# The eighth head pair's exponents transposed by DMA instead of TensorE, with a new search of the order of work

## The chip, the cores and the metric

The kernel runs on one core of a Trainium2 chip. The metric is device microseconds for one execution of the whole program. Before the change it takes 604.61 us, the median of 3 runs (604.5 to 605.64).

## The reference, cut to what matters

```python
# attention with memory: B, H, S, D = 4, 8, 576, 64
scores = q @ k.T / sqrt(D), causal;  a = exp(scores - max) / sum
local  = a @ v
mem    = phi(q) @ M_prev / (phi(q) . z_prev + 1e-6)     # phi = elu + 1
attn   = g * mem + (1 - g) * local                      # g = sigmoid(beta), one per head
# expert: 2304 tokens, d_model 512, d_ff 1536
x   = attn, heads side by side
out = (sigmoid(x @ w_gate) * (x @ w_val)) @ w_out
```

All results are wanted to float32 accuracy; the expert's weights arrive as float64 bit patterns.

## The kernel before, in words

**Groups and pairs.** The 2304 tokens are cut into six groups of 384. Group 0 holds the last 192 tokens of batches 0 and 1, groups 1 to 4 the first 384 tokens of one batch each, group 5 the last 192 of batches 2 and 3. Each group has four pairs of heads, so there are 24 pairs, n = 0 to 23; the eighth pair, n = 7, is the last of group 1. For each pair TensorE makes the scores (`heads`, line 534, and the memory's terms, line 491), VectorE masks them and finds the row extremes (line 603), ScalarE takes the exponents (line 612). A pair of groups 1 to 4 has two items: item 0 of 256 columns and item 1 of 512 columns (384 and 128), each for two heads. The exponents `a` must then be transposed into `at` (`turn`), multiplied with the values (`values`, line 732; two pairs in one step in groups 1 to 4, so pairs 6 and 7 go together), scaled, added to the memory's part, and the result `x` transposed once more (`across`) to feed the expert.

**Two ways to transpose.** Pairs below `XBAR` = 8 use TensorE: 128x128 transposes into PSUM (line 296) and a ScalarE copy from there (line 302). Pairs from `XBAR` on use `planes`: VectorE copies the float32 tile so that its lower and upper 16-bit halves lie apart (line 662), SyncE issues a DMA transpose of 16-bit elements (line 667), and VectorE puts the halves together again (line 662). The same switch decides how `across` transposes `x`.

**Expert.** Every matrix is split into a high and a low part in FP32R, and three products are made for each (line 289). There are 12 blocks of 128 hidden units. Stages: group 0 with blocks 0 to 5, group 1 with blocks 5 to 0, group 0 with blocks 6 to 11, group 1 with 11 to 6, then groups 2 to 5 with all 12. A block has 24 products of 384 columns over four 128-row slices of `x` (slice kd comes from pair kd of the group; in the first block of a stage slice 3 is taken last), a `gate` step (lines 992, 994, 302, 312) and 9 products of 512 columns (`down`). Converting a block's weights from float64 bits takes three conversions of four VectorE and two ScalarE steps each (`convert`; line 881 is the last integer step of each).

**Order.** The program is first written down as 4,634 steps with their dependencies. `Program.issue` then lays each engine's instructions in an order found from planned costs: at each point an engine takes, of its steps that are ready, the one with the lowest number. The number is the step's place in the program, less a `LEAD`, plus what the table `MOVED` adds to it. The order is fixed at build time; on the chip each engine runs its list in that order and waits where a step's inputs are late. For a DMA transpose the plan counts 1.3 us of SyncE, then 1.2 us and the transfer at 380 KB per us, then 0.95 us until an engine may start. At most six `a` and four `at` tiles exist.

**End.** In group 5 the last stage finishes three tiles of 128 rows in the order 2, 0, 1. Tile 2 is halved by ScalarE (line 1037) and goes out in two transfers, tile 0 is halved by VectorE (line 1040), both on SyncE's queue; tile 1 comes in two halves of 256 columns, added up by VectorE (line 1021) and sent by SyncE and ScalarE (line 1024).

Of the kernel before, what the change touches and what calls it, by code (L numbers as in the profile page):

```python
# [11 lines left out]
U16 = mybir.dt.uint16  # L12
AF = mybir.ActivationFunctionType
ALU = mybir.AluOpType
# [5 lines left out]

VC = 66

XBAR = 8

AHEAD = 8

# [11 lines left out]
LINK = 380.0, 1.2  # L38

MOVED = {  # L40
# [42 lines left out]
}  # L83

PE = 2
# [121 lines left out]
def tile_attention_memory_moe(  # L207
# [9 lines left out]
    nc = tc.nc  # L217
    B, HP, _, _ = qk.shape
    D, H = 64, 2 * HP
    NT, DM = out.shape  # L220
# [5 lines left out]
    NG = NT // GT  # L226
# [5 lines left out]
    pg = Program()  # L232
# [65 lines left out]
    def act(n, emit, r, w):  # L298
        pg.add("act", 0.102 + n / 1200.0, emit, r, w)
# [4 lines left out]
    def dve(n, emit, r, w, fast=False):  # L304
        pg.add("dve", 0.083 + n / (1920.0 if fast else 960.0), emit, r, w)
# [99 lines left out]
    for g in range(NG):  # L405
        for p in range(HP):
            u = Pair()
# [248 lines left out]
        recall(n, [(t[:, end:end + 3 * MC].rearrange("p (c j x) -> p c j x", c=3, j=1), k, j, j + 1)  # L656
                   for j, (t, k) in enumerate(sp[0])])

    def planes(src, pl, tl, dst, W, r, pk, lk, key, more=()):

        def move(o, i, r, w):
            dve(2 * W, lambda: nc.vector.tensor_copy(out=o, in_=i), r, w, fast=True)  # L662

        pl, tl = pl[:, :2 * W], tl[:, :2 * W]
        src, dst = (t.bitcast(U16).rearrange("p (w two) -> p two w", two=2) for t in (src, dst))
        move(pl.rearrange("p (two w) -> p two w", two=2), src, r, [pk])
        pg.add("sp", 1.3, lambda: nc.sync.dma_start_transpose(
            out=tl.rearrange("p (x q) -> p x q", q=128), in_=pl), [pk], [lk, *more], 0.75 * W)
        move(dst, tl.rearrange("p (two w) -> p two w", two=2), [lk, *more], [key])

    def crossed(a, nb, at, k):


        W = 128 * nb
        keys = []
        for j, (t, ks, ak) in enumerate(a):
            key = k + (j,)
            o = at[:, W * j:W * j + W]
            end = [ak + ("pad",)] * (nb == 5)
            planes(t[:, :W], o.bitcast(U16), t[:, :W].bitcast(U16), o, W, ks + end, key, ks[0], key, ks[1:] + end)  # L680
            keys.append(key)
            if end:
                pad(t, ak)
        return keys

    def turn(n, c):
        u = pairs[n]
        a = u.a.pop(c)
        nb = -(-sum(W for _, _, W in u.items[c]) // 128)
        at, k = at_r.take()  # L690
        if XBAR <= n:
            u.at[c] = (at, crossed(a, nb, at, k), nb)
            return
        blocks = [(j, i) for j in range(2) for i in range(nb)]
        keys = []
# [246 lines left out]
    def moe(n):  # L942
# [72 lines left out]
        for t in order:  # L1015
# [13 lines left out]
            if not opens:  # L1029
# [3 lines left out]
                for r, q, m in rows(g, t):  # L1033
                    load(out[r:r + m, :], o[q:q + m], 2.1 * m, [ob_k], [])
                continue
            if g < NG - 1 or t != order[1]:
                act(DM, lambda o=o, acc=acc: nc.scalar.activation(
                    out=o, in_=acc, func=AF.Copy, scale=0.5), [acc_k], [ob_k])
            else:
                dve(DM, lambda o=o, acc=acc: nc.vector.tensor_scalar(  # L1040
                    out=o, in0=acc, scalar1=0.5, scalar2=None, op0=ALU.mult), [acc_k], [ob_k])
            if not closes:
                load(halves[g][:, t], o, 256, [ob_k], [("part", g, t)])
                continue
# [110 lines left out]
```

## Time and profile before

| | before |
|---|---|
| median of 3 runs | 604.61 us |
| the profiled execution | 605.47 us |
| its span, first to last instruction | 603.7 us |
| TensorE busy | 592.5 us (98%) |
| VectorE busy | 458.4 us (76%) |
| ScalarE busy | 309.1 us (51%) |
| TensorE's granted clock, mean | 0.998 of full speed |

The profile covers one execution. The span leaves out 1.77 us that the execution's own time has around it. A busy TensorE is one with an instruction in flight: matmuls overlap in its pipeline, so the busy time of a group is larger than the time by which it moves the next one back; the chain of waits gives the latter.

### The profile page before, as it was taken

What the parts mean: (1) busy time and instruction counts of PE and PEld (TensorE: products, weight loads), DVE (VectorE), ACT (ScalarE), POOL (GpSimd) and SP (SyncE); (2) the same over time, 40 slices, a digit from 0 to 9 for tenths busy, and PEclk for the clock granted to TensorE, in tenths of its full rate; (3) what the DMA queues carried; (4) which work ended last, traced back from release to release, by engine and by line L of the source; (5) the groups of instructions that cost most, each with busy time, mean ns of one, the idle gap of its engine ahead of it and who ended that gap; (6) DMA issues with size and microseconds to landing.
All of it is one profiled execution on the core that took longest, in us unless ns stands there. A gap on an engine that the chain in (4) does not pass through costs nothing.

```text
span 603.7 us, 13415 instructions
## 1 busy us (share of the span) xinstructions
PE 592.5 (98%) x5259; PEld 527.5 (87%) x5259; DVE 458.4 (76%) x1183; ACT 309.1 (51%) x616; POOL 9.5 (2%) x59
## 2 busy tenths in 40 slices
PE   7899999999999999999999999999999999999996
PEld 3579888889999899989888989898989889999995
DVE  5898999998988678747868848779999987323433
ACT  7897959554554543244454553454654534223332
POOL 1000000000000000000000000000000000000000
PEclk9999999999999999999999999999999999999999
DMA  8767778697985486536545546655887666222231
GB/s 301 271 215 257 206 223 243 158 264 233 207 252 165 140 191 142 133 106 156 157 132 112 148 135 158 170 127 118 180 217 163 153 135 140 65 70 71 76 98 53
DMA packets 113727, 98.69 MB, mean 163 GB/s; under 512 B 82048, under 2 KB 84352, under 8 KB 113664
## 3 DMA queue, kind: packets, MB, share of 16 engines
q1 hardware_dynamic: 113520, 97.71, 60.0%
q8 instruction: 41, 0.67, 0.5%
q14 instruction: 22, 0.18, 0.1%
q10 hardware_dynamic: 144, 0.13, 0.1%
HBM read 65.84 MB, written 12.58 MB: 130 GB/s over the span
## 4 chain that ended last, share of the span: by engine, by line
PE 93%; DVE 3%; ACT 1%; issue 1%; DMA 1%; DVEq 0%
PE bank L289 77%; PE bank L732 8%; PE bank L534 5%; PE bank L296 2%; PE bank L491 1%; DVE a L603 1%; ACT a L612 1%; DMA kp<-in_qk_dram 1%; ACT at L302 0%; DVE ph L465 0%; DVE xs L312 0%; DVE wt L878 0%; DVE wg L312 0%; DVE sv L312 0%; DVE xm L312 0%
## 5 line engine op out<-in xcount | busy, mean ns | idle before, releaser
L289 PE MATMUL bank<-xh,sv 128*128 128x384 f32 x576 | 162.9, 339 | 0.0
L289 PE MATMUL bank<-xh,wg 128*128 128x384 f32 x576 | 162.0, 338 | 0.0
L289 PE MATMUL bank<-sv,gh 128*128 128x512 f32 x434 | 141.1, 396 | 0.0
L289 PEld LDWEIGHTS bank<-xh,wg 128*128 128x128 f32 x576 | 105.5, 188 | 3.9
L289 PEld LDWEIGHTS bank<-xh,sv 128*128 128x128 f32 x576 | 105.4, 188 | 3.0 <-DVE th L994 0.3
L994 DVE SCALAR_TENSOR_TENSOR th<-th,bank 128x384 f32<-128x384 f32 x72 | 39.7, 552 | 76.8 <-PE bank L289 70.6
L289 PE MATMUL bank<-xl,sv 128*128 128x384 f32 x288 | 97.4, 338 | 0.0
L289 PE MATMUL bank<-xl,wg 128*128 128x384 f32 x288 | 96.3, 336 | 0.0
L289 PEld LDWEIGHTS bank<-sv,gh 128*128 128x128 f32 x434 | 79.6, 188 | 11.7 <-ACT gh L302 0.2
L662 DVE COPY at<-a 128x1024 uint16<-128x1024 uint16 (+2 forms) x144 | 87.4, 640 | 0.8 <-DMA a<-at 0.4
L992 ACT ACTIVATE th<-bank 128x384 f32<-128x384 f32 x72 | 35.4, 491 | 101.3 <-PE bank L289 89.3
L302 ACT CAST gh<-th 128x384 fp32r<-128x384 f32 x72 | 36.9, 512 | 95.1 <-DVE th L994 95.1
L289 PE MATMUL bank<-sv,gl 128*128 128x512 f32 (+1 forms) x217 | 85.2, 395 | 0.0
L312 DVE TENSOR_TENSOR sv<-sv 128x512 fp32r<-128x512 f32 x84 | 54.6, 686 | 8.6 <-ACT sv L302 8.6
L612 ACT ACTIVATE a<-a,st 128x512 f32<-128x512 f32 (+4 forms) x84 | 50.4, 640 | 16.5 <-DVE st L603 16.2
L289 PEld LDWEIGHTS bank<-xl,wg 128*128 128x128 f32 x288 | 54.0, 188 | 2.2
L289 PEld LDWEIGHTS bank<-xl,sv 128*128 128x128 f32 x288 | 54.1, 188 | 1.2
L302 ACT CAST sv<-sv 128x512 fp32r<-128x512 f32 x84 | 47.8, 616 | 9.9 <-DMA sv<-w 9.8
L534 PE MATMUL bank<-kp 64*64 64x256 f32 (+5 forms) x496 | 48.0, 423 | 3.9 <-DMA kp<-in_qk_dram 3.9
L603 DVE CUSTOM_DVE_ANT_0 a<-bank,mask 128x512 f32<-128x512 f32 (+4 forms) x84 | 42.2, 531 | 9.6 <-PE bank L534 8.2
L289 PEld LDWEIGHTS bank<-sv,gl 128*128 128x128 f32 x217 | 40.7, 188 | 8.0
L312 DVE TENSOR_TENSOR gl<-th,gh 128x384 fp32r<-128x384 f32 x72 | 39.9, 554 | 9.7 <-ACT gh L302 9.3
(72 smaller groups left out, 643.3 us busy)
## 6 DMA issues: line engine op xcount, KB each, us to landing
sv<-w SPq DMA_DIRECT2D x42, 512.0 KB, 4.1
wr<-in_w_dram SPq DMA_DIRECT2D x36, 512.0 KB, 4.9
kp<-in_qk_dram SPq DMA_DIRECT2D x32, 384.0 KB, 4.2
w<-wt SPq DMA_DIRECT2D x24, 256.0 KB, 5.0
out_dram<-ob SPq DMA_DIRECT2D x14, 256.0 KB, 2.2
vt<-in_vp_dram SPq DMA_DIRECT2D x8, 330.0 KB, 3.6
vr<-in_vp_dram SPq DMA_DIRECT2D x8, 330.0 KB, 5.1
mb<-in_mz_dram SPq DMA_DIRECT2D x8, 260.0 KB, 5.0
```

The lines of the kernel that those rows point to most:

```text
L289: lambda: nc.tensor.matmul(out=out, lhsT=lhsT, rhs=rhs, start=start, stop=stop), r, w)
L296: pe(0.110, lambda: nc.tensor.transpose(out=out, in_=in_, identity=identity), r, w)
L302: act(n, lambda: nc.scalar.copy(out=out, in_=in_), r, w)
L312: dve(n, lambda: nc.vector.tensor_tensor(out=out, in0=in0, in1=in1, op=op), r, w)
L491: nc.tensor.matmul(out=sp[j][0][m0:m1, at + MC * c:at + MC * c + MC], lhsT=u.ph[r, q:q + m1 - m0], rhs=mem[u.g][e][0][r, u.p, MC * j:MC * ...
L534: nc.tensor.matmul(out=sp[j][0][m0:m1, at:at + k1 - k0], lhsT=kp[r, u.qa + q:u.qa + q + m1 - m0], rhs=kp[r, u.ka + k0:u.ka + k1], start=Tr ...
L603: dve(m + 10, lambda aj=aj, sj=sj, pj=pj, o=o, m=m, mk=mk, b=b0 + k0, i=i: nc.vector.tensor_tensor_reduce(out=aj[:, b:b + m], in0=pj[:, o: ...
L612: act(W + 120, lambda aj=aj, sj=sj, b=b0, W=W, d=depth[x]: nc.scalar.activation(out=aj[:, b:b + W], in_=aj[:, b:b + W], func=AF.Exp, scale ...
L662: dve(2 * W, lambda: nc.vector.tensor_copy(out=o, in_=i), r, w, fast=True)
L732: nc.tensor.matmul(out=out, lhsT=left, rhs=right, start=start, stop=stop)
L992: act(GT, lambda: nc.scalar.activation(out=th, in_=pg_[:, :GT], func=AF.Tanh, scale=0.5), [pg_k], [th_k])
L994: dve(GT, lambda: nc.vector.scalar_tensor_tensor(out=th, in0=th, scalar=1.0, in1=pv[:, :GT], op0=ALU.add, op1=ALU.mult,), [th_k, pv_k], [t ...
```

## The change

`XBAR` becomes 7, so pair 7's exponents and its `x` go through `planes`. A new constant `SHARED` = 8 makes the first copy of `planes` for the exponents of pairs below 8, that is of pair 7 alone, a ScalarE activation (`Copy` on 16-bit integers); the second copy, and both copies for `x`, stay on VectorE. At the end, tile 0 is halved by ScalarE like tile 2, and is sent from ScalarE's queue in one transfer. The table `MOVED` is another one: 484 entries in place of 501, with other offsets nearly everywhere. Step numbers behind pair 7's transposes fall by 3 because of the change. Among the steps of the first pairs, loads 8, 9 and 19 (the memory of group 0 and `beta`) now come before the loads of pair 1's queries and keys (6 and 7); the ScalarE copies of pair 0's transposes (74, 91, 101, 106, 109) and its `values` (110) move 20 places forward; one exponent of pair 1 (79) moves 100 places back; the former preference for pair 0's VectorE steps 112, 113, 114 and 123 is gone.

```diff
-XBAR = 8
+XBAR = 7
+
+SHARED = 8
...
+        -3084740: (4,),
+        -328830: (5,),
...
+        -20: (8, 9, 19, 34, 40, 41, 55, 70, 74, 81, 91, 92, 101, 106, 109, 110, 141, 219, 221, 223, 226, 228, 254,
...
+        100: (79, 3535),
...
-    def planes(src, pl, tl, dst, W, r, pk, lk, key, more=()):
-
-        def move(o, i, r, w):
-            dve(2 * W, lambda: nc.vector.tensor_copy(out=o, in_=i), r, w, fast=True)
+    def planes(src, pl, tl, dst, W, r, pk, lk, key, more=(), shared=False):
+
+        def move(o, i, r, w, shared=False):
+            if shared:
+                act(2 * W + 20, lambda: nc.scalar.activation(out=o, in_=i, func=AF.Copy), r, w)
+            else:
+                dve(2 * W, lambda: nc.vector.tensor_copy(out=o, in_=i), r, w, fast=True)
...
-        move(pl.rearrange("p (two w) -> p two w", two=2), src, r, [pk])
+        move(pl.rearrange("p (two w) -> p two w", two=2), src, r, [pk], shared)
...
-            u.at[c] = (at, crossed(a, nb, at, k), nb)
+            u.at[c] = (at, crossed(a, nb, at, k, n < SHARED), nb)
...
-            if g < NG - 1 or t != order[1]:
-                act(DM, lambda o=o, acc=acc: nc.scalar.activation(
-                    out=o, in_=acc, func=AF.Copy, scale=0.5), [acc_k], [ob_k])
-            else:
-                dve(DM, lambda o=o, acc=acc: nc.vector.tensor_scalar(
-                    out=o, in0=acc, scalar1=0.5, scalar2=None, op0=ALU.mult), [acc_k], [ob_k])
+            act(DM, lambda o=o, acc=acc: nc.scalar.activation(
+                out=o, in_=acc, func=AF.Copy, scale=0.5), [acc_k], [ob_k])
+            if g == NG - 1 and t == order[1]:
+                (r, q, m), = rows(g, t)
+                pg.add("act", 0.4, lambda o=o, r=r: nc.scalar.dma_start(out=out[r:r + 128, :], in_=o), [ob_k], [])
+                continue
```

## Rows read from the trace of the kernel before

**Rows 1.** Chain of waits in order of time, whole span: start us, us, what.

```profile
42.22 1.30 PE bank L296 x9
...
512.69 85.42 PE bank L289 x445
598.14 0.38 DVE at L1040
598.51 0.23 issue
598.75 0.41 DVE at L1021
```

**Rows 2.** Chain of waits, 90 to 140 us.

```profile
95.68 0.58 PE bank L296 x4
...
99.15 0.59 PE bank L296 x4
...
102.17 0.44 PE bank L296 x4
...
103.84 2.95 PE bank L732 x96
...
110.61 0.33 PE bank L296 x3
...
120.69 11.25 PE bank L289 x60
```

**Rows 3.** Busy time by stretch: length, PE, PEld, DVE, ACT, POOL, clock, DMA share, GB/s.

```profile
90.00:105.00 15.00, 15.00 (x179) 13.00 (x173) 14.55 (x47) 13.91 (x30) 0.00 (x0) 1.00 0.83 246
105.00:120.00 15.00, 15.00 (x161) 12.60 (x159) 14.80 (x46) 8.15 (x17) 0.22 (x2) 1.00 0.66 159
120.00:140.00 20.00, 20.00 (x193) 17.88 (x191) 18.12 (x52) 11.37 (x25) 0.00 (x0) 1.00 1.03 290
```

**Rows 4.** Groups by line and shape: busy us, mean ns of one, idle before.

```profile
L662 DVE COPY at<-a 128x1024 uint16<-128x1024 uint16 x80 | 55.3, 718 | 0.7 <-DMA a<-at 0.4
...
L662 DVE COPY at<-a 128x512 uint16<-128x512 uint16 x48 | 20.4, 438 | 0.1
L302 ACT COPY at<-bank 128x512 f32<-128x512 f32 x36 | 20.2, 590 | 4.6 <-PE bank L296 2.7 <-DVE st L603 1.7
L662 DVE COPY xm<-xs 128x768 uint16<-128x768 uint16 x32 | 17.9, 579 | 0.1
...
L651 ACT ACTIVATE a<-a,st 128x384 f32<-128x384 f32 x20 | 11.7, 610 | 1.5 <-DVE st L647 1.5
...
L651 ACT ACTIVATE a<-a,st 128x256 f32<-128x256 f32 x20 | 9.6, 504 | 0.6 <-DVE st L647 0.6
```

**Rows 5.** Line 667, the DMA transposes: issue ns min/median/max, and landing.

```profile
L667 SPq DMA_TRANSPOSE a<-at x72: 1190/1260/2582, 107.8 to 502.7; - x72
...
DMA to landing us min/median/max: 2.4/3.3/7.0
```

**Rows 6.** Tile xs: its DMA transposes' landing, whole span.

```profile
DMA to landing us min/median/max: 2.7/3.1/4.1
```

**Rows 7.** Line 881, the conversions' last integer step, by stretch.

```profile
0.00:101.90 101.90, 12.32 (x18) 1.00 0.75 245
```

**Rows 8.** Line 994, one for each block's gate, by stretch.

```profile
0.00:164.00 164.00, 6.59 (x12) 1.00 0.79 233
```

**Rows 9.** Timeline of PE, 100 to 135 us: start, us, engine, line, operation.

```profile
114.66 0.63 PE L289 MATMUL bank<-sv,gh 128*128 128x512 f32 x2
```

**Rows 10.** Timeline of ACT, 86 to 140 us.

```profile
96.79 1.71 ACT L612 ACTIVATE a<-a,st 128x384 f32<-128x384 f32 x4
```

**Rows 11.** Timeline of all engines, 598 us to the end.

```profile
598.08 1.80 SPq L320 DMA_DIRECT2D out_dram<-at  x3
598.14 0.69 DVE L1040 TENSOR_SCALAR at<-bank 128x512 f32<-128x512 f32 x1 [1.68 <-PE bank L289]
...
599.58 0.38 ACTq L1024 DMA_DIRECT2D out_dram<-at  x1
599.93 0.70 SPq L1024 DMA_DIRECT2D out_dram<-at  x1
```

**Rows 12.** Busy time by stretch, before TensorE is full; columns as in rows 3.

```profile
6.10:23.00 16.90, 15.12 (x226) 9.67 (x223) 13.43 (x47) 13.83 (x27) 0.47 (x4) 1.00 0.80 289
23.00:42.20 19.20, 18.57 (x253) 12.50 (x252) 19.16 (x64) 18.63 (x38) 0.47 (x4) 1.00 0.77 271
```

More of the change, by code (lines that the diff above doesn't have):

```diff
@@ L669, in planes, with crossed @@
         move(dst, tl.rearrange("p (two w) -> p two w", two=2), [lk, *more], [key])
-    def crossed(a, nb, at, k):
+    def crossed(a, nb, at, k, shared):
         W = 128 * nb
@@ L679, in crossed @@
             end = [ak + ("pad",)] * (nb == 5)
-            planes(t[:, :W], o.bitcast(U16), t[:, :W].bitcast(U16), o, W, ks + end, key, ks[0], key, ks[1:] + end)
+            planes(t[:, :W], o.bitcast(U16), t[:, :W].bitcast(U16), o, W, ks + end, key, ks[0], key, ks[1:] + end, shared)
             keys.append(key)
```

88 rows, old and new, of the table MOVED are left out of this document.

## The prediction, made before the change was run

> **What bounds the kernel now.** I read the chain of waits first, in order of time. From 42.22 us to 598.14 us it never leaves TensorE [rows 1]: in those 556 us an instruction taken from TensorE shortens the program by the slot that it held in the stream, as long as nothing else is made late. Before 42.22 us and after 598.14 us other engines set the pace. Then I read the busy time of each engine by stretch, around pair 7. TensorE is full in each, and VectorE nearly so: it idles 0.45 us of 15 from 90 to 105 us and 0.20 us of 15 from 105 to 120; ScalarE idles 1.09 us and then 6.85 us [rows 3]. So work that is moved off TensorE here lands on engines with little room, and the question is whether what they then do late is anything that TensorE waits for. Last come the start, where VectorE works 19.16 of 19.20 us from 23 to 42.2 but leaves 3.47 us unused before that [rows 12], and the end, a short chain of copies and DMA issues [rows 1, 11].
>
> **The change part by part.**
>
> *Removed from TensorE.* The order of the steps places pair 7's twelve transposes of exponents in the three pieces of four behind each other in the chain, 0.58 + 0.59 + 0.44 us, and those of its `x` in the last piece of three, 0.33 us [rows 2]: 1.94 us. The cheapest of these pieces cost 0.11 us for a transpose; fifteen at that price are 1.65 us, which is the lower bound. The dearest is 0.59 / 4 = 0.1475, fifteen are 2.21, the upper one. I take 1.9.
>
> *ScalarE.* Three copies out of PSUM at 0.590 us go, 1.77 us [rows 4]. Four moves of 16-bit elements come: two of 512 and two of 1024 per partition. The trace has none on this engine. Two exponents, of 384 and 256 columns, take 610 and 504 ns, so 0.83 ns per element [rows 4]; from the copy's 590 ns at 512, 1024 elements come to 590 + 512 x 0.83 = 1.02 us, and the four to 3.2 us (estimate). From below, the 1024-element move of VectorE, 0.718 us, with 0.438 us for 512, gives 2.3 us; from above, every 512 elements as dear as a copy plus half of that again gives 6 x 0.885 = 5.3 us, for the case that reading every second 16-bit word slows the engine. I take 3.2, so ScalarE has 1.4 us more (0.5 to 3.5). From 90 to 105 us it has 1.09 us free, and then 6.85 [rows 3], so it costs nothing by itself; without that cover it would delay the exponents of pair 8.
>
> *VectorE.* Four moves come that put the halves together, 2 x 0.438 + 2 x 0.718 = 2.31 us, and for `x` two of 0.579, 1.16 us [rows 4]; nothing goes. With 3.47 us more against 0.65 us free between 90 and 120 [rows 3], some 2.8 us of its work slides behind 120. What can slide: all 18 conversions that the first six blocks need are started by 101.9 us [rows 7], and by 164 us only the twelve gates of the first two stages have run [rows 8]. The conversions after 101.9 are therefore for blocks that TensorE first uses after 164 us, over 40 us behind this stretch, and from 120 to 140 us VectorE has 1.88 us free [rows 3]. I take 0 for it, and keep 2.8 us as the bound, for the case that urgent work slides instead.
>
> *SyncE and latency.* Five DMA transposes come, 1.26 us of the queue each and 3.3 us from issue to landing [rows 5]. What they make late is worked out from the last exponents: these end at 96.79 + 1.71 = 98.50 us [rows 10]. Two ScalarE moves end at 99.5 and 100.5; the second transpose leaves behind the first at about 100.9 and lands at 104.2; VectorE needs 0.72 us, so `values` of pairs 6 and 7 can start at 104.9 in place of 103.84 [rows 2] and end 2.95 us later, at 107.9. Before, the transposes of pair 7's `x` began 3.8 us after the end of `values` (110.61 against 106.79 [rows 2]); the same now gives 111.7, then 0.58 for a move, 3.1 for the landing [rows 6], 0.58 for the second move, and a cast and a subtraction of 384 elements, for which I put 0.58 each (the price of the move): about 117.1 us. What waits for that is slice 3 of the first block of the second stage. Its first products ran at about 114.3 us, just before 114.66 [rows 9], and would run at 112.4 with 1.9 us less in front. But everything that TensorE did from 114.66 to 120.69 us [rows 9, 2], 6.0 us, needs nothing of pair 7: the last products of the first stage, slices 0 to 2 of the other half, scores of pair 9. The order can put that first, which covers until 118.4 us. So the lateness is hidden with 1.3 us to spare: cost 0. SyncE's other loads are few there; I put nothing for them.
>
> A rule speaks against this part: the Trainium skill, VectorE: DVE Perf Modes, "Rules for kernel authors", says of a 128x128 transpose: "Use TensorE if PSUM dest is OK; xbar DMA otherwise", and the section on the three transpose paths gives 390 ns for TensorE and 1309 ns for the DMA (a bf16 block). The trace agrees on the latency, 3.3 us to landing against a slot of 0.11 to 0.15 us [rows 5, 2]. By that page's figures fifteen blocks would be 15 x (1.309 - 0.390) = 13.8 us slower where nothing hides them (estimate from the page); by the rows the same step is a gain of 1.9 us while TensorE is the bound and the latency is covered.
>
> *The end.* SyncE's queue holds three transfers from 598.08 for 1.80 us, and only then, at 599.93, issues the first half of tile 1, which had been added up at 598.75 + 0.41 = 599.16 [rows 11, 1]. With tile 0 on ScalarE's queue SyncE is free at 598.08 + 1.20 = 599.28, 0.65 us sooner; and VectorE need not do the 0.69 us of tile 0 before the halves. ScalarE copies tile 0 until about 598.75 (0.59) and issues it in 0.38 to 0.70 us [rows 11], so that it can issue the second half at 599.2 to 599.5, before at 599.58. The later of the two queues decides: 0.4 to 0.65 us are gained. I take 0.5.
>
> *The start.* VectorE is full from 23 us on and on the chain there, so a gain has to come from the 3.47 us that it idled before [rows 12]; that is the bound of the gain. What the edits do fits: the memory's loads earlier let pair 0's memory terms fill idle time, and pair 0's copies and `values` go ahead of pair 1's exponents. Against it, pair 1's keys are issued three loads later; three issues of the end take 1.80 us [rows 11], which I take as the bound of the loss. I take a gain of 0.7, a little under the middle of -1.8 and +3.47.
>
> *Sum.* -1.9 - 0.5 - 0.7 = -3.1 us. The profiled execution took 605.47 us, so 602.4 there; the median of the runs shown lies 0.86 us lower, at 604.61, so **601.5 us** against that. The extremes of the terms: -2.2 - 0.65 - 3.5 = -6.4 on one side; -1.65 - 0.4 + 1.8 + 2.8 = +2.55 on the other. A measurement of this kernel can tell about 0.2%, 1.2 us, from no change.
>
> **The rivals.**
>
> *VectorE gives it back.* If the planner lets urgent work slide (the last conversions of block 5, the gates), the 2.8 us that find no room between 90 and 120 us come back as waits of TensorE: -3.1 + 2.8 = -0.3, **604.3 us**. For it: two engines are at 97% and 93% there [rows 3]. Against it: the conversions among that work are not due yet [rows 7, 8]. A start that loses instead of gaining ends in the same place: -1.9 - 0.5 + 1.8 = -0.6, 604.0 us.
>
> *Pair 7's `x` is late (slower).* Two DMA transposes stand in series between the exponents and slice 3, and the order is fixed by planned landings. The slack is 1.3 us, so TensorE begins to wait when the two land 1.3 us later in sum than 3.3 and 3.1. The longest landing of the exponents' transposes is 7.0 us and of `x` 4.1 us [rows 5, 6]. If both happen here, 4.7 us more, TensorE waits 3.4 us in front of slice 3; with ScalarE's moves at the upper price, 0.885 x 4 - 2.04 = 1.5 us later, it waits 4.9: -3.1 + 4.9 = +1.8, **606.4 us**. It decides the sign when the wait passes 3.1 us. For it: the stretch around 105 us has DMA at 66 to 83% [rows 3] and SyncE's queue is in order. Against it: the median landing, and the plan counts about 4.4 us from issue to use, more than the median. The rule of the Trainium skill above (VectorE: DVE Perf Modes) amounts to this rival: latency decides there, and not the slot.
>
> *The change of order does nothing.* Within the TensorE-bound stretch another order can't gain, only lose; if the start's edits merely swap equal waits, the sum is -2.4, 602.2 us; this lies inside the forecast.
>
> **How the numbers follow.** Forecast (transposes and end gained, start between nothing and 2.5 us): 0.64, 599.5 to 603.3. VectorE or the start gives it back, within 0.2%: 0.21. `x` late or another stall, slower: 0.15. The range that leaves out no more than 2 in 10 is 599.3 to 605.2. Faster 0.64, same 0.21, slower 0.15.
>
> **What would show it.** Right: the groups of line 296 shrink by 12 and 3 instructions, and line 667 has 4 transposes more for `a` and 1 for `x`; the chain stays on TensorE from about 42 us (or sooner) to the end with no wait between 100 and 125 us; `values` of pairs 6 and 7 starts later against the exponents but its successors don't wait; the last transfers are issued at most 1.2 us after TensorE's last product. Wrong: a wait of TensorE for VectorE or a DMA between 100 and 125 us; ScalarE's 16-bit moves above 1.5 us; the chain leaving VectorE for good later than 42.22 us; or code loading or loads falling otherwise somewhere in the new order.

## The result: slower by 0.56%, and the profile after

The changed kernel takes 608.43 us (median of 4 runs, 608.19 to 608.70), the kernel before 604.97 us on the same chip (median of 4 runs, 604.50 to 605.64; the three shown above gave 604.61): ratio 1.0056, interval 1.0045 to 1.0068. I had forecast 601.5 us, in a range of 599.3 to 605.2. The profiled execution took 608.43 us with a span of 606.6 us.

Chain of waits of the changed kernel, whole span (start us, us, what). Lines have moved: 289 is now 299, 296 is 306, 732 is 745, 662 is 675, 667 is 680, 994 is 1007; line 673 is the new ScalarE move.

```profile
42.45 3.18 PE bank L745 x104
...
75.66 2.95 PE bank L745 x96
...
100.28 6.78 DMA a<-at
...
125.01 9.82 DMA a<-at x2
136.70 4.41 PE bank L299 x20
142.63 3.02 PE bank L745 x96
```

Before, the chain stayed on TensorE from 42.22 us on [rows 1]. Now it leaves TensorE at 90.86 us, runs over ScalarE's moves, the last DMA transpose of pair 7, VectorE's queue and the last two of pair 9, and comes back at 136.70 us. The milestones say when the time goes, though only roughly, as TensorE's own order is another one too. `values` of pair 2 begins at 42.45 us in place of 43.52 (which the chain of before puts behind its 1.30 us from 42.22 [rows 1]); that of pairs 6 and 7 at 105.68 in place of 103.84 [rows 2]. Where the chain of before showed nothing but TensorE, TensorE now waits. These are all waits of TensorE between 40 and 600 us, first in the kernel before, then in the changed kernel (us in total, times, longest):

```profile
PE bank L296 <- DVE st L603: 0.2, 1, 0.2
```

```profile
PE bank L745 <- issue: 1.5, 1, 1.5
PE bank L299 <- ACT gh L312: 0.8, 1, 0.8
PE bank L299 <- DVE th L1007: 0.5, 1, 0.5
PE bank L299 <- DVE xm L322: 0.2, 1, 0.2
```

Busy time by stretch in the changed kernel, with the columns and stretches of [rows 3] and [rows 12]:

```profile
90.00:105.00 15.00, 14.48 (x110) 12.40 (x107) 14.18 (x46) 13.56 (x27) 0.00 (x0) 1.00 1.09 229
105.00:120.00 15.00, 14.17 (x179) 11.22 (x178) 13.34 (x43) 7.69 (x16) 0.22 (x2) 1.00 0.64 187
120.00:140.00 20.00, 19.68 (x140) 16.81 (x139) 17.50 (x42) 9.74 (x20) 0.00 (x0) 1.00 0.97 249
6.10:23.00 16.90, 16.90 (x243) 11.81 (x240) 14.06 (x55) 14.65 (x30) 0.47 (x4) 1.00 0.89 330
```

VectorE was given more work between 90 and 120 us, and gets less done there than before: it is busy for 27.52 us in place of 29.35 [rows 3], because it stands and waits. At the same time the DMA share from 90 to 105 us rises from 0.83 [rows 3] to 1.09, while the bytes per second fall from 246 to 229 GB/s: the transposes fill the DMA engines and move little. TensorE's clock is at its upper level (1.00, 2.4 GHz) in every stretch, so it explains nothing.

What VectorE stands for is in its timeline (start us, us, engine, line, operation, and in brackets the idle time ahead and what ended it):

```profile
107.09 0.76 DVE L675 COPY at<-a 128x1024 uint16<-128x1024 uint16 x1 [1.62 <-DMA a<-at]
107.74 0.54 DVE L322 TENSOR_TENSOR gl<-th,gh 128x384 fp32r<-128x384 f32 x1
...
109.27 0.54 DVE L1007 SCALAR_TENSOR_TENSOR th<-th,bank 128x384 f32<-128x384 f32 x1
...
134.86 0.75 DVE L675 COPY at<-a 128x1024 uint16<-128x1024 uint16 x1 [1.67 <-DMA a<-at]
135.50 0.68 DVE L894 SCALAR_TENSOR_TENSOR wt<-wr,wt 128x512 int32<-128x512 int32 x1
136.09 0.55 DVE L1007 SCALAR_TENSOR_TENSOR th<-th,bank 128x384 f32<-128x384 f32 x1
...
139.63 0.42 DVE L657 CUSTOM_DVE_ANT_0 a<-bank,mask 128x256 f32<-128x256 f32 x1
```

The queue is in order: behind the move that waits for its transpose stand gate steps (lines 322 and 1007) whose inputs are there. The same two places in ScalarE's timeline and then in TensorE's:

```profile
109.85 0.51 ACT L312 CAST gh<-th 128x384 fp32r<-128x384 f32 x1 [0.43 <-DVE th L1007]
...
136.68 0.51 ACT L312 CAST gh<-th 128x384 fp32r<-128x384 f32 x1 [4.09 <-DVE th L1007]
```

```profile
110.41 1.66 PE L299 MATMUL bank<-sv,gh 128*128 128x512 f32 x6 [0.81 <-ACT gh L312]
...
142.63 1.62 PE L745 MATMUL bank<-vt,at 128*64 128x66 f32 x48 [1.51 <-issue]
```

At 110.41 us `down` waits for a gate that is late by VectorE's 1.62 us. At 142.63 us the page names no releaser, but the rows above lead to it: the gate at 136.09 is late, ScalarE waits 4.09 us for it, VectorE's next steps run behind, and the masks of scores from 139.63 us on, which read them out of the PSUM bank, end only just before `values` can start.

Line 680, the DMA transposes, issued from 92 to 107 us, pair 7's four (issue ns min/median/max; landing us):

```profile
L680 SPq DMA_TRANSPOSE a<-at x4: 1237/1546/2322, 93.0 to 100.3; - x4
...
DMA to landing us min/median/max: 4.3/6.1/7.2
```

I had put 3.3 us, the median over the whole span [rows 5]. Over the whole span it is now 3.4 us; here it is 6.1.

The groups of second (and some first) moves, to be held against [rows 4]:

```profile
L675 DVE COPY at<-a 128x1024 uint16<-128x1024 uint16 x82 | 57.2, 719 | 4.9 <-DMA a<-at 4.7
...
L675 DVE COPY at<-a 128x512 uint16<-128x512 uint16 x50 | 21.3, 439 | 1.5 <-DMA a<-at 1.4
```

Two more instructions in each, and the price of one is what it was. The idle time in front of the larger ones goes from 0.7 to 4.9 us.

The end, to be held against [rows 11]:

```profile
601.17 1.17 SPq L330 DMA_DIRECT2D out_dram<-at  x2
...
602.38 0.59 SPq L1037 DMA_DIRECT2D out_dram<-at  x1
602.43 0.36 ACTq L1037 DMA_DIRECT2D out_dram<-at  x1
```

SyncE's half follows its other transfers at once, 0.49 us after TensorE's last product (601.61 + 0.28 us). Yet the span ends 4.75 us after that product, where it was 4.84.

### The profile page after: what moved, and what is told of

It is laid out like the page before. It is cut to its first block, busy times and chain, and to the rows that moved or that the text cites. A ratio compares the mean times of both kernels' runs of the same rounds, so it can differ in the third digit from the quotient of the medians.

```text
span 606.6 us, 13411 instructions
## 1 busy us (share of the span) xinstructions
PE 593.3 (98%) x5244; PEld 527.2 (87%) x5244; DVE 461.2 (76%) x1188; ACT 312.8 (52%) x618; POOL 11.8 (2%) x59
## 4 chain that ended last, share of the span: by engine, by line
PE 82%; DVE 8%; ACT 4%; DMA 3%; issue 1%; DVEq 0%
PE bank L299 67%; PE bank L745 7%; PE bank L544 5%; DMA a<-at 3%; PE bank L306 2%; DVE at L675 2%; DVE a L613 1%; ACT a L622 1%; ACT at L312 1%; PE bank L501 1%; DVE kq_wt L322 1%; DVE th L1007 1%; DMA kp<-in_qk_dram 1%; DVE xm L675 1%; ACT at L673 1%
## 5 line engine op out<-in xcount | busy, mean ns | idle before, releaser
L299 PE MATMUL bank<-xh,wg 128*128 128x384 f32 x576 | 163.8, 339 | 0.3 <-DVE xm L322 0.2
L299 PE MATMUL bank<-sv,gh 128*128 128x512 f32 x434 | 138.6, 394 | 0.9 <-ACT gh L312 0.8
L675 DVE COPY at<-a 128x1024 uint16<-128x1024 uint16 (+2 forms) x148 | 91.0, 639 | 6.6 <-DMA a<-at 6.1
L299 PE MATMUL bank<-sv,gl 128*128 128x512 f32 (+1 forms) x217 | 83.3, 395 | 0.0
L544 PE MATMUL bank<-kp 64*64 64x256 f32 (+5 forms) x496 | 49.8, 429 | 4.4 <-DMA kp<-in_qk_dram 4.3
```

The costliest lines, as they stand in the source:

```text
L299: lambda: nc.tensor.matmul(out=out, lhsT=lhsT, rhs=rhs, start=start, stop=stop), r, w)
L544: nc.tensor.matmul(out=sp[j][0][m0:m1, at:at + k1 - k0], lhsT=kp[r, u.qa + q:u.qa + q + m1 - m0], rhs=kp[r, u.ka + k0:u.ka + k1], start=Tr ...
```

## The experiments

In experiments 4 to 8 the order of every engine is written out as the changed kernel has it, and only the steps named are moved, so that nothing else shifts; in experiment 10 it is written out as in experiment 3. In experiments 1 to 3 and 9 the plan lays out the order anew from the offsets named. Ratios are to the kernel before, on the same chip. Line numbers shift from kernel to kernel.

**1. The first pairs' order alone.**

```diff
 MOVED = {                      # the old table, but for steps 0 to 479
+        -3084740: (4,),
+        -328830: (5,),
...
```

> The kernel before with the changed table's offsets for the first 480 steps alone (the first pairs' new order); pair 7's exponents stay on TensorE, the end is the old one. Theory T1 (the loss of the change is made by pair 7's late DMA transposes, the start is a true gain that was lost behind): values of pairs 4 and 5 begin 2 to 2.5 us before the 77.95 us of before, and the whole takes 1.6 to 2.4 us less, about 603.0 us against 604.97. Theory T2 (the new order of the first pairs only borrows time that later steps give back, and the order itself makes the loss): values of pairs 4 and 5 are early, but those of pairs 8 and 9 are not before 138.0 us, and the time is 604.5 us or more.

Measured: 604.52 us, ratio 0.9991 (0.9981 to 1.0000). `values` of pairs 4 and 5 begin at 76.8 us, 1.1 us sooner; in other profiles with these first steps they begin between 75.2 and 77.0 us, so one profile can't size a gain of this kind. The start gains about 0.5 us, at the edge of what can be measured, and keeps it. That is near my forecast (0.7) and far from T1's 1.6 to 2.4 us; T2's limits are just met (`values` of pairs 8 and 9 begin at 138.0 us, 604.52 us against 604.5 or more), but its reason, time that later steps give back, is not: they begin 0.4 us sooner than before, and the span is 1.4 us shorter.

**2. The same, with the end.**

```diff
-                dve(DM, ...)               # halve tile 0
+                act(DM, ...)
+            pg.add("act", 0.4, lambda o=o, r=r: nc.scalar.dma_start(out=out[r:r + 128, :], in_=o), [ob_k], [])
```

> The run with the first pairs' new order alone, and tile 0 of the end by ScalarE as in the change. By the changed kernel's trace (last product to end of span 4.75 us against 4.84) the end is worth about 0.1 us: 0.0 to 0.3 us less than without it. By my forecast it is worth 0.4 to 0.65 us. If the end is worth the forecast, the last product to the end of the span falls to 4.4 us or less.

Measured: ratio 0.9992 (0.9981 to 1.0003): the end is worth nothing that can be measured. The trace shows why. Transfers of the run without the new end, then of the run with it: SyncE's issue of tile 1's half, and the landing of both halves.

```profile
598.84 0.44 SPq L1028 DMA_DIRECT2D out_dram<-at  x1
...
DMA to landing us min/median/max: 2.5/2.6/2.6
```

```profile
597.85 0.58 SPq L1028 DMA_DIRECT2D out_dram<-at  x1
...
DMA to landing us min/median/max: 3.0/3.1/3.3
```

TensorE's last product ends 0.33 us sooner in the second, SyncE's half is issued 0.99 us sooner: the 0.65 us that I forecast for the issue came. But five transfers now leave within 1.3 us instead of 1.9, and each of the two halves lands 0.5 to 0.7 us later. That the closer issue is the reason is not shown: all nine profiles with the new end have 3.0 to 3.3 us, six with the old end 2.5 to 2.6, but that of the kernel before, with the old end too, has 2.9 to 3.1.

**3. The new order, pair 7 still on TensorE.**

```diff
-XBAR = 7
+XBAR = 8
 MOVED = {                      # the new offsets for steps below 1350, the old ones beyond
```

> Pair 7's exponents and x on TensorE as before, but the changed table's offsets for all steps up to the end of the disputed stretch (the first 1350 steps), the old table's offsets beyond, and the old end. Theory T1 (pair 7's DMA path makes the loss): no wait of VectorE for a DMA transpose of pair 7, values of pairs 8 and 9 at 136 to 138.5 us, time 602.5 to 604.2 us. Theory T2 (the searched order of 90 to 145 us makes the loss whichever way pair 7 takes): values of pairs 8 and 9 not before 141 us, time 606 us or more.

Measured: ratio 1.0003 (0.9994 to 1.0013), and in a later run 1.0011 (1.0000 to 1.0023). Theory T1 gave 602.5 to 604.2 us and T2 606 or more: 605.1 to 605.3 us lies between, and so do the `values` of pairs 8 and 9, which begin at 139.7 us (T1: 138.5 at the latest, T2: not before 141). The new order without the new path loses the start's gain, 0.7 to 1.2 us, but it doesn't make the 3.4 us.

**4. Two of VectorE's moves later.** Step 817 is the second move of pair 7's last exponents, 1113 that of pair 9's.

```diff
 VectorE's order:
-  817, 838 (gl of a gate), 792, 983,
+  838, 792, 983, 817,
...
-  1113, conversion steps, 1061 (th of a gate), 1063 (gl),
+  conversion steps, 1061, 1063, 1113,
```

> The changed kernel with its order of every engine written out as it is, and two of VectorE's instructions moved: the second move of pair 7's last exponents stands behind the subtraction of a gate step that it stood in front of (a few VectorE steps later), and the second move of pair 9's last exponents behind the last steps of another gate. Nothing else differs. Theory T1 (TensorE waits because VectorE, in order, stands in front of a late transpose and what is queued behind it, the gates and the release of the score bank, comes late): TensorE's waits of 0.81 us at 110.4 and of 1.51 us at 142.6 shrink to under 0.5 us together, values of pairs 8 and 9 at 140 to 141 us, time 605.5 to 607.2 us. Theory T2 (the order of TensorE's own work loses the time): values of pairs 8 and 9 at 142.6 as in the changed kernel and 608.0 us or more.

Measured: 605.63 us, ratio 1.0012 (1.0003 to 1.0022). Two instructions that an in-order engine runs some steps later take back 0.44%, 2.7 us of 3.4 (1.9 of 2.6 against the second run of the changed kernel, in experiment 5). TensorE's waits from 40 to 600 us in this kernel:

```profile
PE bank L499 <- DVE th L1207: 0.5, 1, 0.5
PE bank L945 <- issue: 0.5, 1, 0.5
PE bank L499 <- DVE gl L522: 0.4, 1, 0.4
PE bank L499 <- DVE xm L522: 0.2, 1, 0.2
```

The 0.8 us are gone and the 1.5 us have become 0.5, as T1 said. Pair 7's last two transposes land 5.2 us after issue here too, so it isn't they that got faster: VectorE's waits for transposes from 90 to 150 us fall from 4.7 to 1.2 us.

**5. Which of the two moves.** Each alone, with the changed kernel run again beside them.

> Of the two moves of the run that moved both (ratio 1.0012), only that of pair 7's last exponents stands later in VectorE's order; pair 9's stays. Theory T1a (each late transpose makes its own wait of TensorE): the wait of 0.81 us at 110 goes and that of 1.5 us in front of the values of pairs 8 and 9 stays, values of pairs 8 and 9 about 0.8 to 1.2 us sooner than in the changed kernel, ratio 1.003 to 1.0045. Theory T1b (the wait at pair 9 is only a follow-up of pair 7's lateness): both waits go, ratio 1.001 to 1.002.

> Only the second move of pair 9's last exponents stands later in VectorE's order; pair 7's stays where the change has it. Theory T1a: the wait of 1.5 us in front of the values of pairs 8 and 9 shrinks to 0.5 us or less, that of 0.8 us at 110 stays, ratio 1.002 to 1.0035. Theory T1b: the wait at 110 stays and what VectorE does late behind it keeps the other wait too, ratio 1.005 or more.

> The changed kernel once more, on the same chip as the three runs beside it: ratio 1.0045 to 1.0068 as measured, with VectorE's waits of 1.6 to 1.7 us for the transposes of pairs 7 and 9 and TensorE's waits of 0.8 and 1.5 us behind them in the profile.

Measured: pair 7's move alone 1.0050 (1.0034 to 1.0067), pair 9's move alone 1.0018 (1.0004 to 1.0031), the changed kernel again 1.0043 (1.0028 to 1.0059). So pair 9's move carries it, 1.5 us of 2.6; the two intervals just touch. Pair 7's move alone gains nothing that can be measured. Neither T1a nor T1b came out as written. TensorE's waits in the run with pair 7's move alone, the two longest, and then all in the run with pair 9's alone:

```profile
PE bank L945 <- issue: 1.5, 1, 1.5
...
PE bank L945 <- DVE at L875: 0.9, 1, 0.9
```

```profile
PE bank L499 <- DVE th L1207: 0.5, 1, 0.5
PE bank L945 <- issue: 0.4, 1, 0.4
PE bank L499 <- DVE xm L522: 0.2, 1, 0.2
```

With pair 7's move later, `values` of pairs 6 and 7 wait 0.9 us for that move itself: it can stand in front of the gates, or be late for its own reader. And the 0.8 us at 110 us is not there in the second profile of the changed kernel (there it waits 0.7 us in all for gates, once 0.5), nor with pair 9's move alone, so it comes and goes with the landings.

**6. Transfers behind pair 7's transposes.**

```diff
 SyncE's order:
-  701 (store of weights), 980 (load of keys), 756, 813, 816 (transposes of pair 7),
+  756, 813, 816, 701, 980,
```

> The changed kernel with its order written out, and two of SyncE's transfers (a store of converted weights and a load of keys, issued at 94.97 and 95.48 us between the DMA transposes of pair 7) moved behind pair 7's last transpose. Theory T1 (pair 7's transposes land late because they queue behind these transfers): the transposes issued at 95.95, 98.67 and 100.28 us, which land after 7.19, 5.46 and 6.78 us in the changed kernel, land after 3 to 5 us; the wait of VectorE for them, 2.15 us at 103 to 107, falls under 0.7 us, TensorE's wait of 0.81 us at 110.4 goes, and the time is 606.5 to 607.8 us (pair 9's wait of 1.51 us stays). Rival T3 (a DMA transpose under load is slow by itself, whatever stands before it in the queue): landings stay at 5 us and more and the time at 608.0 to 608.8 us.

Measured: ratio 1.0060 (1.0043 to 1.0077), no gain. The transposes did what T1 said. Pair 7's transposes in this run, then the weight loads behind them (those land after 5.2 to 5.4 us in the changed kernel), then ScalarE's wait:

```profile
DMA to landing us min/median/max: 3.7/4.0/4.9
```

```profile
L530 SPq DMA_DIRECT2D wr<-in_w_dram x2: 414/418/423, 103.5 to 105.6; - x2
...
DMA to landing us min/median/max: 6.4/6.5/6.6
```

```profile
110.09 0.66 ACT L1087 ACTIVATE wt<-wr 128x512 f32<-128x512 f32 x1 [2.96 <-DMA wr<-in_w_dram]
110.66 0.49 ACT L512 CAST gh<-th 128x384 fp32r<-128x384 f32 x1
```

Now ScalarE stands in front of a weight load, with the gate's cast behind it, and TensorE waits 1.3 us for that cast. What now stands behind the transposes lands late in their place. So here the queue's order chose who is late; T1's part on the queue is right, its 0.6 to 1.9 us of gain fell.

**7. Both edits.**

> Both edits together: the two second moves later in VectorE's order, and the two transfers behind pair 7's last transpose. If both undo the same wait (T1: one cause, late landing, seen from two sides), the second adds little to the first: 605.0 to 605.8 us, as the moves alone (ratio 1.0012). If they are separate losses the gains add up: about 604 us. If the loads that are now late are needed soon, it is slower than the moves alone: above 606 us.

Measured: ratio 1.0033 (1.0021 to 1.0045), 606.75 us: the third of the cases that I had named, worse than the moves alone. The loads that are now late are needed soon, as experiment 6 shows.

**8. Pair 7's first moves on VectorE.**

```diff
-SHARED = 8
+SHARED = 7
```

> The changed kernel with its order written out, but pair 7's four first moves (the 16-bit halves apart) are done by VectorE in place of ScalarE, in their old places in the order. My forecast's term for ScalarE (0, hidden by its idle time) and the theory that VectorE is the tight engine between 90 and 120 us say: VectorE has 2.3 us more there and is in front of the gates, so the time is 1 to 3 us more than the changed kernel's 608.4, 609.4 to 611.4. Rival: VectorE only uses up the 2.15 us that it stood waiting for the transposes anyway, so 608.0 to 609.0.

Measured: ratio 1.0081 (1.0060 to 1.0103), 609.26 us, a little under what my forecast's view gave and above the rival's 609.0: by the ratios 1.5 us more than the changed kernel, and 2.3 more than its second run. ScalarE is the right engine for these moves; VectorE's standing time doesn't absorb them. The interval overlaps with the changed kernel's first one (1.0045 to 1.0068), so the size is rough.

**9. The path alone, with the old offsets.** The plan makes another order of the old offsets too: TensorE's and VectorE's steps stand in other places from 95 to about 200 us.

> The change of path alone: pair 7 by DMA transposes with ScalarE's first moves, but the old table's offsets carried over to the same steps, and the old end. My forecast's terms for the path, 1.9 us of TensorE gained and all else hidden, give 602.9 us. Theory T1 says that the late transposes of pair 7 stop VectorE in any order that was not made for them: VectorE waits for DMA transposes by 2 us or more between 100 and 140 us, and the time is 606 to 610 us.

Measured: 608.63 us, ratio 1.0064 (1.0048 to 1.0081); T1 holds in time. VectorE waits 1.3 us for transposes, less than the 2 us that I expected; TensorE's one large wait from 40 to 600 us is

```profile
PE bank L536 <- DVE xl L314: 1.8, 1, 1.8
```

It ends at 118.13 us. Less than 1 us later TensorE's granted clock falls to its lower level (0.50, 1.2 GHz) and stays there for 6.8 us (the columns of [rows 3]):

```profile
119.06:125.88 6.82, 6.82 (x27) 5.39 (x20) 6.43 (x23) 4.42 (x9) 0.52 (x2) 0.50 1.13 304
```

At half the clock these 6.8 us hold 3.4 us of work at the upper level (estimate), more than the wait itself. The fall is not needed for the loss: this execution took 609.84 us at a mean clock of 0.994, one more had 0.994 and 610.08 us, and the other four, at 0.997 to 0.998, took 607.5 to 608.9 us, still 2.7 to 4.2 above the kernel before. So the path costs about as much with the old offsets as in the order searched for it, but not by the same waits. Nor does this run part T1 from the rival that VectorE lacks room: behind the 1.3 us of standing VectorE has no gap from 108.41 us until the step that TensorE waits for.

**10. The load of the transposes, with nobody waiting for it.** To the kernel of experiment 3 four DMA transposes are added for pair 7, then three more.

```diff
         u.at[c] = (at, keys, nb)
+        if n == 7:
+            W = 128 * nb
+            for j, (t, ks, ak) in enumerate(a):
+                pg.add("sp", 1.3, lambda t=t, j=j: nc.sync.dma_start_transpose(
+                    out=t[:, :W].bitcast(U16).rearrange("p (x q) -> p x q", q=128),
+                    in_=at[:, W * j:W * j + W].bitcast(U16)), keys, ks, 0.75 * W)
```

> The run with pair 7 on TensorE and the changed table's offsets up to the end of the stretch (605.1 us, ratio 1.0003), its order written out, with four DMA transposes added for pair 7 (two of 512 and two of 1024 16-bit elements, from its transposed tile back into its exponents' tile, which nobody reads any more), so that SyncE and the DMA carry the load of the change while no engine waits for it. The output stays the reference's. If the load itself is the loss (the loads of weights behind it come late, and with them the gates), the ratio is 1.002 to 1.005 and ScalarE or VectorE wait for weight loads that they did not wait for without. If only VectorE's standing in front of the transposes is the loss, the ratio stays within 1.0003 +- 0.001.

> The run with four idle DMA transposes for pair 7, and three more beside them (of 512 16-bit elements each, into places that nobody reads), in the order of the run with pair 7 on TensorE. The output stays the reference's. If the load on SyncE and the DMA by itself costs what the four seemed to (1.1 us, ratio 1.0021 against 1.0003), half as much load again and three more issues add to it: ratio 1.003 or more, with ScalarE's waits for weight loads above the 2.8 us that they took with four. If the load costs nothing by itself, the ratio is that of the control beside it within 0.001.

> The control on the same chip: pair 7 on TensorE with the changed table's offsets up to the end of the stretch. Ratio 1.0003 +- 0.001 as before; values of pairs 8 and 9 about 64.0 us behind those of pairs 4 and 5.

Measured: with four 1.0021 (1.0007 to 1.0035), with seven 1.0048 (1.0030 to 1.0065), the control 1.0011 (1.0000 to 1.0023). With four, the profile shows no wait of TensorE but one of 0.3 us that the control has too, and its interval overlaps the control's: 0.6 us, not certain. With seven the load alone costs 2.2 us. Waits of ScalarE, VectorE and TensorE in that run:

```profile
ACT wt L1095 <- DMA wr<-in_w_dram: 5.3, 2, 3.0
```

```profile
DVE wt L1097 <- ACT wt L1095: 2.1, 2, 1.6
```

```profile
PE bank L506 <- DVE xs L522: 0.9, 1, 0.9
PE bank L499 <- ACT gh L512: 0.4, 1, 0.4
```

The control's ScalarE waits 0.7 us for weight loads there, with four transposes 2.8 us, with seven 5.3 us. So in this order the stretch had room for about four more transposes on the DMA, not for seven.

## Why the prediction was wrong, point by point

- **The step that failed** is "SyncE and latency": "it lands at 104.2", "SyncE's other loads are few there; I put nothing for them", "So the lateness is hidden with 1.3 us to spare: cost 0". I took the median landing over the whole span, 3.3 us, where the four transposes took 4.3 to 7.2. The DMA share of 0.83 in [rows 3] was the sign: a stretch that is nearly full doesn't give the median. Two transfers that are issued just ahead of the second transpose, moved behind the last, shorten the later landings from 5.5 to 7.2 us to 3.7 to 4.9 (experiment 6). What stands in place of the 0 is 1.5 to 2.7 us for VectorE's waits for late transposes (experiments 4 and 5). It is seen at pair 9: neither moving pair 7's move alone (experiment 5) nor landing its transposes sooner, where other loads came late instead (experiment 6), gained anything that can be measured.
- **VectorE, "I take 0"**, failed with it, though not as I had bounded it. I asked whether 2.8 us of work would find room. Whether it would have is not shown: VectorE stood for 2.2 us between 90 and 120 us and got less done, and 2.3 us more work there cost 1.5 to 2.3 us (experiment 8). What I left out is that a second move is an in-order wait, and that the gates stand behind it. Moving two of them takes back 2.7 us (experiment 4; 1.9 against the second run of the changed kernel).
- I looked for the lateness only behind pair 7. The larger loss is at **pair 9**, which went by DMA before as well. Its last transposes landed 6.0 and 7.0 us after issue before the change too (the 7.0 us is the longest of [rows 5]); there no gate stood behind the move with so little slack. In the new order one does (experiment 5). That is of the new order together with the new path: with pair 7 on TensorE and the same offsets TensorE has no such wait (experiment 3).
- **ScalarE** was right: two moves at 0.63 us and two at 1.06, 3.4 us where I put 3.2. The group in the changed kernel:

```profile
L673 ACT ACTIVATE at<-a x4: 631/850/1062, 92.3 to 99.2; 128x512 uint16<-128x512 uint16 x2, 128x1024 uint16<-128x1024 uint16 x2
```

- **TensorE's 15 transposes** are gone (152 to 140 and 24 to 21 in the groups of line 306); their slot of 1.9 us was not measured by itself.
- **The end**, 0.5 us forecast, is worth 0 (0.9992 against 0.9991): the issue came 0.65 us sooner and the landing took it back. **The start**, 0.7 forecast, is worth 0.5.
- **The rivals.** "VectorE gives it back" had the right engine and the right victims, the gates, but by lack of room and with 2.8 us as its limit. "Pair 7's `x` is late" had the right cause, landings at the long end (7.2 us against the 7.0 of [rows 5]), but for that `x` TensorE did not wait: the 0.2 us for `xm` end at 120.73 us with a step that reads a memory term out of PSUM. Its condition, a wait of 3.1 us in sum, is nearly met by the 3.0 in the table of waits, at places that I hadn't looked at; by my sum that would only have cancelled the gain, and the kernel is 3.4 us slower.
- **The account.** From the ratios, with 1 at 604.8 us: start -0.5, end 0, new order 0.7 to 1.2, the load of the four transposes 0 to 0.6, VectorE standing in front of two of them 1.5 to 2.7. TensorE's waits that are left with both moves later are 1.6 us (experiment 4), 1.3 more than the control's 0.3. With the forecast 1.9 us of TensorE off, this makes 1.1 to 3.4, and 2.6 to 3.4 was measured. The terms may overlap (the load makes some of the waits that are left). The table of waits doesn't hold the whole loss either. From the first `values` of pair 2 to the last product TensorE takes 559.4 us (42.45 to 601.89) where it took 555.3 (43.52 to 598.81), 4.1 us more; the waits listed are 2.8 us more, and the fifteen transposes that are gone should have taken off 1.65 us or more (0.11 us each [rows 2]). So some 3 us went between TensorE's instructions where no wait is listed, and what made them stays open; with both moves later the same stretch takes 557.0 us (43.60 to 600.60). The runs don't part the new order's share any finer: why it loses the start's gain with pair 7 on TensorE stays open. No version here beats the kernel before by more than can be measured: the start alone, at 0.9991, is the best.

The Trainium skill, VectorE: DVE Perf Modes, "Rules for kernel authors", prefers TensorE for a 128x128 transpose where PSUM will do as its destination; by this case's runs that was the better choice for pair 7 in the order as searched, at ratios of 1.0003 to 1.0011 (with the old end and the old later offsets) against 1.0043 to 1.0056. With two moves placed later the DMA path is at 1.0012, level with it (experiment 4). The 3.3 us that the prediction set beside the page's figure are the landing of a whole transpose of four or eight 16-bit blocks, so they agree with it in direction and not in size; and the fifteen float32 blocks go by DMA as thirty 16-bit ones, of which the prediction's estimate from the page counted half.

## What to carry to other kernels

Here the median landing of the whole run misled: a transfer's latency is to be read in the stretch where it will run, among the loads that stand ahead of it in its queue, and not over the whole run. When work goes from a full engine to a DMA, list what is queued on the in-order engine behind the instruction that will wait for the landing: that queue is late, and not only the reader of the data. If an order is planned ahead, leave the wait's worst landing in front of nothing urgent; moving one such instruction behind a gate was worth about 1.5 us here, where the path was forecast to gain 1.9. And a list of an engine's waits should be held against the time that its whole stream took: here it left some 3 us out.

## What the runs showed of the hardware

- DMA transposes fill the engines without moving much. From 92 to 107 us of the changed kernel 3,314 of 4,210 packets are under 512 bytes (144 of 1,370 in the kernel before), and with the queue's transfers at 108% of the engines' time the rate is 237 GB/s (76% and 242 GB/s before).
- On one queue the order moves the lateness about: with two transfers moved behind pair 7's transposes, three of the four transposes land 1.7 to 3.0 us sooner after issue, the weight loads behind them 1.2 us later, 6.4 to 6.6 after issue in place of 5.2 to 5.4, and the time stays (1.0060 against 1.0056).
- Output transfers landed later when they were issued closer together, with one exception: two halves of 256 columns after 2.5 to 2.6 us when they left 0.37 us apart behind three others (in the profile of the kernel before, 2.9 to 3.1), after 3.0 to 3.3 us when five left within 1.3 us.
- TensorE's granted clock can fall inside a long program: in the profile of experiment 9 it went from 1.00 to 0.50 at 119.06 us, behind a wait of 1.8 us that had ended at 118.13, and was back at 125.88. Products of 384 columns that started 0.17 us apart before started 0.32 us apart. Behind the wait of 1.5 us in the changed kernel it did not fall.
